# Linear attention followed by a spectral mix on one core: the first sixteen loads of q, k and V are written out in another order, and two of them are issued by ScalarE

## The chip, the cores and the metric

The kernel runs on one core of one Trainium2 chip. The metric is device time in microseconds (us) of one execution: before the change the median of three runs was 445.62 us, with 444.76 the lowest and 445.84 the highest.

## What is computed

Inputs are q, k and v of shape (batch 8, heads 8, sequence 576, 64), a projection `w_phi` (64 x 128), and the weights of the second part: `moe_w_r` and `moe_w_i` (64 modes of 512 x 512) and `moe_w_ch` (512 x 512). All are float32. The first part is attention with exponential features and no softmax:

```python
def phi(x):
    proj = x @ w_phi
    proj = proj - max(abs(proj))                 # over the 128 features
    return concatenate([exp(proj), exp(-proj)])  # 256 features
kv  = einsum('bhsf,bhsd->bhfd', phi(k), v);  z = phi(k).sum(sequence)
att = (phi(q) @ kv) / (phi(q) . z + 1e-6)
```

Its result, with the heads put side by side (512 columns), is the `x` of the second part. A real Fourier transform runs over the sequence; each of the first 64 modes is multiplied by its own complex 512 x 512 matrix; the inverse transform gives `y`; and with `u = x + y` the output is `u + relu(u @ w_ch)`, shape (8, 576, 512), float32.

## The kernel before

**Stages.** The attention part is a list `S` of 32 stages, each with two (batch, head) pairs, one on SBUF partitions 0 to 63 (the lower half) and one on 64 to 127 (the upper half). The main loop runs over n = 0 to 33, and in turn n it starts stage n, carries on stage n-1 and finishes stage n-2, so the three overlap. For a stage, q and k in bf16 are transposed on TensorE (`transp`, L196 and L199), copied out by VectorE (L205), projected (`feat_tok` L214, `feat_q` L223), their largest absolute value is taken by VectorE (`absmax`, L248), the exponentials are made by ScalarE (`exps` L255 to L263, `ekq` L270), V is scaled by GpSimd (`vscale`, L285 and L290), and matmuls and VectorE operations build the quotient into `xs_all` (L301 to L351).

**Loads of q, k and V.** V is loaded in float32 for every stage by SyncE (SP), through `load`, into four rotating buffers `vn` (L122 and L127). For stages 0 and 1 alone, `load` also brings q and k in float32 (`qn` and `kn`, two buffers each); `casts` (L154) turns those into bf16, on VectorE for stage 0 and on GpSimd for stage 1. A stage of this early kind takes two batches, so each of its tiles is loaded by two DMAs of 144 KB: the lower half first, then the upper. Sixteen such DMAs make up q, k and V of stages 0 and 1 and V of stages 2 and 3. From stage 2 on, q and k come in pairs of stages through `load_qk` (L138, L143): DMAs issued by GpSimd that cast to bf16 on the way.

**Weights.** The mode matrices come in 32 groups. `weights(k)` makes the four DMAs of a group (L169, L175; 512 KB as written in bf16, read as float32), each to one half of the partitions, lower half first, and GpSimd issues them. A list written by hand, `plan`, says how many of these DMAs and which `load_qk` GpSimd issues in each turn of the main loop, ahead of that turn's `vscale`. Three buffers rotate, so the issue of a group waits until the group three before it has been multiplied (`mode_mm`, L426 and L438). After the main loop, a second loop handles the remaining groups; then the inverse transform, the last matmul and the output follow.

**Order around the change.** The program order is written by hand and each engine works through its own list in order. Before the main loop it is: q and k of stage 0 on SP; the first group's list of weight DMAs; `setup` (ScalarE issues the two DMAs of `w_phi`, L486 and L487; GpSimd issues the first two weight DMAs, `load_qk` of stages 2 and 3, and the other two weight DMAs; VectorE and ScalarE make the Fourier table, L500 to L526; VectorE casts `w_phi` to `w2`, L527); V of stage 0, then q, k and V of stage 1 on SP; the casts of stage 0 on VectorE and of stage 1 on GpSimd, with small memsets between; the transposes of stage 0. V of stages 2 and 3 is loaded at the head of turns 0 and 1. DMAs of SP and ScalarE share eight completion semaphores in rotation, so the ninth of them waits until the first has landed, and so on.

Of the kernel before, what the change touches and what calls it, by code (L numbers as in the profile page):

```python
# [10 lines left out]
F32 = mybir.dt.float32  # L11
# [7 lines left out]
B_, H_, S_, D_ = 8, 8, 576, 64  # L19
# [7 lines left out]
def kernel(  # L27
# [11 lines left out]
    nc = tc.nc  # L39
# [43 lines left out]
    pa_in = pa_in_cm.__enter__()  # L83
# [7 lines left out]
    def qk_pair(pool, i):  # L91
        return [pool.tile([128, 2, 10, D_], BF16, name=f"{nm}2_{i}") for nm in "qk"]
# [3 lines left out]
    pa_first = pa_first_cm.__enter__()  # L96
# [4 lines left out]
    S = [dict(bs=(2 * i, 2 * i + 1), h=h, xt=1 - h) for h in range(2) for i in range(B_ // 2)]  # L101
    S += [dict(b=b, g=g, xt=g % 2) for g in range(1, H_ // 2) for b in range(B_)]
    N = len(S)
# [7 lines left out]
    after = [3] * 4 + [7] * 4 + [15] * 8 + [23] * 8 + [31] * 8  # L111
    W = {}

    def load(st, which="qkv"):
        for nm, src, bufs in (("q", q, 2), ("k", k, 2), ("v", v, 4)):
            if nm not in which or (nm != "v" and st["n"] >= 2):
                continue
            pool = pa_in if nm == "v" else pa_first
            t = pool.tile([128, 9, D_], F32, name=f"{nm}n", tag=f"{nm}n", bufs=bufs)
            if "bs" in st:  # L120
                for x in range(2):
                    nc.sync.dma_start(  # L122
                        t[64 * x:64 * x + 64],
                        src[st["bs"][x], st["h"]].rearrange("(p j) d -> p j d", j=9))
            else:
                b, g = st["b"], st["g"]
                nc.sync.dma_start(  # L127
                    t, src[b, 2 * g:2 * g + 2].rearrange("h (p j) d -> (h p) j d", j=9))
            st[nm] = t


    def load_qk(m):
        st = S[2 * m]
        for nm, src, t in zip("qk", (q, k), qk2s[m % 3]):
            if "bs" in st:
                for x in range(2):
                    b = st["bs"][x]
                    nc.gpsimd.dma_start(  # L138
                        t[64 * x:64 * x + 64, :, 0:9, :],
                        src[b:b + 3:2, st["h"]].rearrange("u (p j) d -> p u j d", j=9))  # L140
            else:
                b, g = st["b"], st["g"]
                nc.gpsimd.dma_start(  # L143
                    t[:, :, 0:9, :],
                    src[b:b + 2, 2 * g:2 * g + 2].rearrange("u h (p j) d -> (h p) u j d", j=9))
            for x in range(2):
                S[2 * m + x][nm + "b"] = t[:, x]

    def casts(st, eng, which="qk"):
        n = st["n"]  # L150
        for nm, t in zip("qk", qk2s[0]):
            if nm in which:
                st[nm + "b"] = t[:, n % 2]
                eng.tensor_copy(t[:, n % 2, 0:9, :], st[nm])  # L154

    def weights(k):
        g, gi = groups[k]
        W[k] = wt = {}
        for ri, w in ((0, moe_w_r), (1, moe_w_i)):
            for y in range(2):  # L160
                def issue(ri=ri, w=w, y=y):
                    if y == 0 and k == 0:
                        wt[ri] = Yacc.rearrange("p a e -> p (a e)").bitcast(BF16).rearrange(
                            "p (r m e) -> p r m e", r=2, m=8)[:, ri]
                    elif y == 0:
                        wt[ri] = pw.tile([128, 8, DMODEL], BF16, name=f"w{'ri'[ri]}", tag=f"w{ri}")
                    t = wt[ri][64 * y:64 * y + 64]
                    if gi >= 0:
                        nc.gpsimd.dma_start(  # L169
                            t.rearrange("p (m i) e -> p m (i e)", i=2),  # L170
                            w[8 * gi + y:8 * gi + 8:2, g * 128:(g + 1) * 128, :].rearrange(
                                "m (p i) e -> p m (i e)", i=2))
                    else:
                        m0 = 16 * (-1 - gi) + 8 * y
                        nc.gpsimd.dma_start(  # L175
                            t, w[m0:m0 + 8, g * 64:(g + 1) * 64, :].rearrange("m p e -> p m e"))
                due.append((k, issue))
# [130 lines left out]
    def kv_cp(st):  # L308
        kvzF = pa_mid.tile([128, 2, 130], BF16, name="kvzF", tag="kvzF")
        nc.scalar.copy(kvzF, st["kvz"][:, :, 0:130])  # L310
        st["kvzF"] = kvzF
# [248 lines left out]
    m_in = 2  # L560
    pa_last_cm = None
    with tc.manual_schedule():
        load(S[0], "qk")
        weights(0)
        k_in = 1
        setup()
        load(S[0], "v")
        load(S[1])
        casts(S[0], nc.vector)
        casts(S[1], nc.gpsimd, "q")  # L570
        for t in AAs:
            nc.gpsimd.memset(t[:, 0, :, 1152:1216], 1.0)
        for t in e2s:
            nc.gpsimd.memset(t[64:128, :, NCH - 1:NCH], 1.0)
        casts(S[1], nc.gpsimd, "k")

        pa_first_cm.__exit__(None, None, None)
        pa_last_cm = tc.tile_pool(name="pa_last", bufs=1)
        pa_last = pa_last_cm.__enter__()
        qk2s[2] = qk_pair(pa_last, 2)  # L580
        for t in qk2s[2]:
            nc.gpsimd.memset(t[:, :, 9, :], 0.0)
        transp(S[0], "q")
        transp(S[0], "k")
        for n in range(N + 2):
            cur = S[n] if n < N else None
            prev = S[n - 1] if 0 <= n - 1 < N else None
            old = S[n - 2] if 0 <= n - 2 < N else None
            nxt = S[n + 1] if n + 1 < N else None
            if n + 2 < N:  # L590
                load(S[n + 2])
            if cur:
                feat_tok(cur, "k", "pB")
                feat_q(cur)
            if psY is not None:
                mode_sum(k_out, psY)
                psY = None
                k_out += 1
            if cur:
                rem_mm(cur)  # L600
                absmax(cur, "k")
                absmax(cur, "rem")
                exps(cur, "q")
            if nxt:
                transp(nxt, "q")
            if prev:
                kv_mm(prev)
                kv_cp(prev)
            if cur:
                ekq(cur, "k")  # L610
            for c in plan[n - 1] if n else "":
                if c == "q":
                    load_qk(m_in)
                    m_in += 1
                elif c == "c":
                    nc.gpsimd.dma_start(wchb, moe_w_ch.rearrange("(dc p) e -> p dc e", p=128))
                else:
                    if not due:
                        assert k_in < max(k_out, 1) + NW
                        weights(k_in)  # L620
                        k_in += 1
                    issue_weights(1)
            if cur:
                vscale(cur)
            if n == 6:
                make_identity(nc, ident_f)
            if nxt:
                transp(nxt, "k")
            if cur:
                exps(cur, "k")  # L630
                exps(cur, "rem")
            if prev:
                num_mm(prev, 1)
                numer(prev, 0)
                num_mm(prev, 0)
                numer(prev, 1)
                numer(prev, 2)
            if old:
                x_mm(old)
            e = n - (N + 2 - N_EARLY)  # L640
            if e >= 0:
                sTe = flip_early(e)
            if cur:
                feat_tok(cur, "q", "pA")
                absmax(cur, "q")
                ekq(cur, "q")
            if n == 0:
                forward_matrix()
            if n in (1, 2):
                zeros(2 - n)  # L650
            if 10 <= n < 10 + NCH:
                inverse_matrix(n - 10)
            if n in (9, 15):
                zeros_late(1 if n == 9 else 0)
            if e >= 0:
                times_w_early(e, sTe)
            if k_out < len(at) and n == at[k_out]:
                assert after[k_out] + 2 <= n < (10, 18, 26, 99)[min(k_out // 4, 2) if k_out < 16 else 3]
                assert not due_of(k_out)
                psY = mode_mm(k_out)  # L660
# [147 lines left out]
    for n, (b, c, late) in enumerate(seq):  # L808
        u = dict(b=b, c=c, late=late == 1, half=c == 4, cut=n == 0, n=n,
                 tags=("T0", "T1") if n % 2 == 0 else ("T2", "T3"),  # L810
                 pool=(lambda: psumA) if n % 2 == 0 else (lambda: psum))
# [43 lines left out]
    with tc.manual_schedule():  # L855
        flip_x()
        flip_x()
        for k in range(k_out, 31):
# [8 lines left out]
            if yst is not None:  # L867
                if gi % 2 == 0:
                    sY = pb.tile([128, 4, 2, 128], BF16, name="sY", tag="sY")
                transposed(yst, sY, gi, (((0, 4), psum.tile([128, 4, 128], BF16, name="ptY",  # L870
                                                            tag="tr")),))
# [19 lines left out]
        for m, eng in ((-2, nc.sync), (-1, nc.gpsimd), (-3, nc.sync)):  # L891
            t, gi, a, b = Yst[m]
# [6 lines left out]
        st = [pb.tile([128, DMODEL], BF16, name=f"st{h}", bufs=1) for h in range(2)]  # L899
# [10 lines left out]
        for b, eng in ((1, nc.sync), (4, nc.gpsimd), (5, nc.sync), (6, nc.gpsimd),  # L910
                       (2, nc.sync), (7, nc.gpsimd), (3, nc.gpsimd)):
            j = b % 4
# [47 lines left out]
```

## Time and profile before

The profile is of one execution, which took 445.59 us, within 0.01% of the median; its span, from the first instruction to the last, is 443.8 us, and 1.8 us lie around it.

| what | value |
|---|---|
| time of the profiled execution | 445.59 us |
| span | 443.8 us |
| median of the runs | 445.62 us (444.76 to 445.84) |
| busy share: TensorE, VectorE, ScalarE, GpSimd | 70%, 66%, 61%, 49% |
| bytes written by DMA, packets | 97.86 MB, 60997 |
| queue q0 (DMAs issued by GpSimd) | 76.69 MB, 95.9% of 16 engines' span |
| queue q1 (DMAs issued by SP) | 20.35 MB, 13.3% |
| queue q10 (DMAs issued by ScalarE) | 0.07 MB, 0.1% |

PE is TensorE, PEld its weight loads, DVE is VectorE, ACT is ScalarE and POOL is GpSimd; SPq, ACTq and POOLq are their queues' instructions, such as the issue of a DMA. L122 is line 122 of the kernel. The profile counts a DMA's bytes as written: a DMA that casts float32 to bf16 reads twice what it writes. "DMA share" in the stretch tables adds up the time of packets over 16 engines, and packets of one engine overlap, so a full stretch shows more than 1.

### The profile page before, as it was taken

To read this page: it belongs to the slowest core of one execution; us is meant where nothing else is said; L and a number is where in the kernel's file an instruction comes from. 1 tells how busy PE (TensorE), PEld (TensorE's weight loads), DVE (VectorE), ACT (ScalarE), POOL (GpSimd) and SP (SyncE) were. 2 spreads that over 40 slices of the span, in tenths; PEclk is the share of its full clock that TensorE was granted. 3 is DMA by queue.
4 is the path that set the end of the run, shared out by engine and by line. 5 is a ranking of instruction groups with operands and counts; after the bars stand their busy time and mean duration, and the time that the engine had idled before them with its cause. 6 is when DMAs were issued, how large, how long until landed. Compare 5 with 4: busy or idle time off the path is not lost.

```text
span 443.8 us, 11840 instructions
## 1 busy us (share of the span) xinstructions
PE 310.9 (70%) x4981; PEld 201.5 (45%) x4981; DVE 293.7 (66%) x417; ACT 270.8 (61%) x567; POOL 218.1 (49%) x303
## 2 busy tenths in 40 slices
PE   0666667775767777677453767766897776789993
PEld 0455555554555655465342544433443333344441
DVE  4778879989888687878744796664232356363783
ACT  3676687886886875688633866663363254353762
POOL 6776448585566656547534554442222222200893
PEclk9999899899896596868966787888999699889997
DMA  8999999999999999999999999999999999993598
GB/s 190 243 228 218 220 228 217 229 218 218 230 221 223 221 233 221 223 233 222 223 220 222 222 222 211 211 212 211 211 211 211 211 211 211 211 207 74 183 363 328
DMA packets 60997, 97.86 MB, mean 221 GB/s; under 512 B 3936, under 2 KB 28992, under 8 KB 60944
## 3 DMA queue, kind: packets, MB, share of 16 engines
q0 software_dynamic: 51952, 76.69, 95.9%
q1 hardware_dynamic: 8832, 20.35, 13.3%
q8 instruction: 39, 0.64, 0.5%
q10 hardware_dynamic: 160, 0.07, 0.1%
q14 instruction: 14, 0.11, 0.1%
HBM read 163.64 MB, written 9.44 MB: 390 GB/s over the span
## 4 chain that ended last, share of the span: by engine, by line
DMA 55%; DVE 18%; PE 14%; issue 4%; ACT 4%; POOL 2%; ACTq 0%; SPq 0%; DVEq 0%; POOLq 0%
DMA wi<-in_moe_w_i_dram 35%; DMA wr<-in_moe_w_r_dram 9%; DMA k<-in_k_dram 8%; DVE mkq L248 7%; DVE nd L337 2%; DVE xs_all L351 2%; ACT AA L255 2%; DVE tB L330 2%; PE psB L785 2%; PE psB L778 2%; DMA kn<-in_k_dram 2%; PE psA L799 2%; PE ptr L199 1%; POOL vaug L285 1%; DMA fs<-in_w_phi_dram 1%
## 5 line engine op out<-in xcount | busy, mean ns | idle before, releaser
L285 POOL TENSOR_TENSOR vaug<-vn,ee 128x576 bf16<-128x576 f32 x64 | 72.7, 1156 | 45.7 <-ACT ee L270 43.6
L255 ACT ACTIVATE AA<-psT 128x1024 bf16<-128x1024 f32 x64 | 62.0, 1021 | 24.9 <-PE psT L223 24.2
L169 POOL DMA_DIRECT2D wr<-in_moe_w_r_dram x48 | 29.7, 620 | 78.4 <-PE psY L438 21.0
L277 ACT ACTIVATE e<-mkq 64x4 f32<-64x4 f32 (+1 forms) x128 | 26.3, 206 | 60.1 <-DVE mkq L248 57.7
L259 ACT ACTIVATE AA<-psk 128x1024 bf16<-128x1024 f32 x64 | 61.4, 1009 | 0.0
L169 POOL DMA_DIRECT2D wi<-in_moe_w_i_dram x48 | 29.9, 625 | 45.0 <-DMA wi<-in_moe_w_i_dram 13.5
L248 DVE TENSOR_REDUCE mkq<-psk 128x8 f32<-128x1024 f32 x32 | 38.7, 1211 | 0.7 <-PE psk L214 0.7
L248 DVE TENSOR_REDUCE mkq<-psq 128x8 f32<-128x1024 f32 x32 | 38.9, 1217 | 0.4 <-PE psq L214 0.3
L438 PE MATMUL psY<-wi,XT 128*32 128x512 bf16 x192 | 19.1, 477 | 26.1 <-DMA wi<-in_moe_w_i_dram 26.1
L707 ACT CAST xw<-psW 128x512 bf16<-128x512 f32 x34 | 19.8, 586 | 25.5 <-PE psW L705 25.2
L438 PEld LDWEIGHTS <-XT 128*32 128x32 bf16 x384 | 14.6, 173 | 45.8 <-issue 23.1
L705 PE MATMUL psW<-wchb,sT 128*128 128x512 bf16 x136 | 33.3, 389 | 0.0
L205 DVE COPY kT<-ptr 128x640 bf16<-128x640 bf16 x32 | 15.7, 492 | 25.3 <-PE ptr L199 25.3
L330 DVE TENSOR_TENSOR tB<-psNB,e 128x650 f32<-128x650 f32 x32 | 26.6, 832 | 8.8 <-PE psNB L320 8.4
L320 PEld LDWEIGHTS <-AA 128*128 128x128 bf16 x640 | 28.8, 110 | 7.6 <-issue 7.1
L697 DVE COPY sT<-pt 128x1024 bf16<-128x1024 bf16 x17 | 11.8, 692 | 30.5 <-PE pt L694 30.5
L223 PE MATMUL psT<-qT,w 64*128 64x512 bf16 x64 | 15.4, 471 | 23.4 <-DVE mkq L248 23.3
L199 PE MATMUL ptr<-ident_b,k 128*128 128x128 bf16 x160 | 18.1, 259 | 19.6 <-DVE qT L205 17.7
L351 DVE TENSOR_TENSOR xs_all<-nd,rden 128x640 bf16<-128x640 f32 x32 | 30.4, 951 | 1.1
L301 PE MATMUL kvz<-vaug,AA 64*128 64x65 bf16 x1152 | 28.8, 208 | 2.3 <-DVE Yacc L453 1.5
L337 DVE TENSOR_TENSOR nd<-psNA,tB 128x650 f32<-128x650 f32 x32 | 26.7, 835 | 3.8 <-DVE tB L330 0.5
L301 PEld LDWEIGHTS <-AA 64*128 64x128 bf16 x1152 | 24.5, 106 | 6.9 <-issue 2.3
(142 smaller groups left out, 726.6 us busy)
## 6 DMA issues: line engine op xcount, KB each, us to landing
wr<-in_moe_w_r_dram POOLq DMA_DIRECT2D x62, 512.0 KB, 18.9
wi<-in_moe_w_i_dram POOLq DMA_DIRECT2D x62, 512.0 KB, 18.7
out_dram<-of SPq DMA_DIRECT2D x15, 512.0 KB, 4.7
vn<-in_v_dram SPq DMA_DIRECT2D x24, 288.0 KB, 6.0
q<-in_q_dram POOLq DMA_DIRECT2D x12, 288.0 KB, 17.4
k<-in_k_dram POOLq DMA_DIRECT2D x12, 288.0 KB, 17.6
vn<-in_v_dram SPq DMA_DIRECT2D x16, 144.0 KB, 7.0
Yacc<-in_moe_w_r_dram POOLq DMA_DIRECT2D x2, 512.0 KB, 8.7
```

Of the source, the lines that this page charges most:

```text
L169: nc.gpsimd.dma_start(t.rearrange("p (m i) e -> p m (i e)", i=2), w[8 * gi + y:8 * gi + 8:2, g * 128:(g + 1) * 128, :].rearrange("m (p i) ...
L248: nc.vector.tensor_reduce(out=o, in_=i, axis=AX.X, op=ALU.max, apply_absolute_value=True)
L255: nc.scalar.activation(AA[:, 0, ab, 0:1024].rearrange("f (x j p) -> f j x p", j=2, p=64), st["psT"].rearrange("f j (x p) -> f j x p", p=64 ...
L259: nc.scalar.activation(AA[:, 1, ab, 0:1024].rearrange("p (c j f) -> p j c f", c=4, j=2), st["psk"], ACT.Exp, scale=sc)
L285: nc.gpsimd.tensor_tensor(out=vaug[:, ab, :, 0:64], in0=st["v"], in1=ee[:, ab, :].unsqueeze(2).to_broadcast([128, 9, D_]), op=ALU.mult,)
L301: nc.tensor.matmul(kvz[:, hh, ab * 65:(ab + 1) * 65], lhsT=AA[r, 1, ab, 128 * j:128 * j + 128], rhs=vaug[r, ab, j, :], start=(j == 0), sto ...
L320: nc.tensor.matmul(p[:, hh, 65 * c:65 * c + 65], lhsT=AA[:, 0, ab, x:x + 128], rhs=kvzF[:, hh, ab * 65:(ab + 1) * 65], start=True, stop=True,)
L330: nc.vector.tensor_tensor(out=tB, in0=st["psNB"], in1=e2.unsqueeze(3).to_broadcast([128, 2, NCH, 65]), op=ALU.mult,)
L337: nc.vector.tensor_tensor(out=nd, in0=st["psNA"], in1=st["tB"], op=ALU.add)
L351: nc.vector.tensor_tensor(out=xo, in0=nd[:, :, :, 0:64], in1=rden.to_broadcast([128, 2, NCH, 64]), op=ALU.mult,)
L438: nc.tensor.matmul(psY[32 * j:32 * j + 32, :], lhsT=XT[:, 16 + 32 * ri:48 + 32 * ri, 32 * i + 4 * gi + j], rhs=wt[ri][:, 2 * j + i, :], st ...
L705: nc.tensor.matmul(ps, lhsT=sT[:, x, dc, :], rhs=wchb[:, dc, :], start=(dc == 0), stop=(dc == 3))
```

## The change

The sixteen first loads are written out in one function, called where `load(S[0], "qk")` stood, ahead of everything else. The lower half of q and then of k of stage 0 goes to SP, and the upper halves of the same two to ScalarE, ahead of its two DMAs of `w_phi`. Then SP issues all remaining upper halves (V of stage 0; q, k and V of stage 1; V of stages 2 and 3), and after them the lower halves in the same order. The sixteen DMAs are the same as before in size, source and destination; 14 are now SP's and 2 ScalarE's. The calls of `load` for stages 0 to 3 go; from stage 4 on V is loaded as before. On TensorE, VectorE and GpSimd the order of instructions is the same in both kernels.

```diff
+    def first_loads():
+        for n in range(4):
+            for nm, bufs in (("q", 2), ("k", 2), ("v", 4)):
+                if nm == "v" or n < 2:
+                    pool = pa_in if nm == "v" else pa_first
+                    S[n][nm] = pool.tile([128, 9, D_], F32, name=f"{nm}n", tag=f"{nm}n", bufs=bufs)
+
+        def half(eng, n, nm, x):
+            src = dict(q=q, k=k, v=v)[nm]
+            eng.dma_start(S[n][nm][64 * x:64 * x + 64],
+                          src[S[n]["bs"][x], S[n]["h"]].rearrange("(p j) d -> p j d", j=9))
+
+        for nm in "qk":
+            half(nc.sync, 0, nm, 0)
+            half(nc.scalar, 0, nm, 1)
+        for x in (1, 0):
+            for n, nm in ((0, "v"), (1, "q"), (1, "k"), (1, "v"), (2, "v"), (3, "v")):
+                half(nc.sync, n, nm, x)
...
     with tc.manual_schedule():
-        load(S[0], "qk")
+        first_loads()
         weights(0)
         k_in = 1
         setup()
-        load(S[0], "v")
-        load(S[1])
         casts(S[0], nc.vector)
...
-            if n + 2 < N:
+            if 4 <= n + 2 < N:
                 load(S[n + 2])
```

More of the change, by code (lines that the diff above doesn't have):

```diff
@@ L112, with load @@
     W = {}
[L114 to L126, printed above, removed]
-                nc.sync.dma_start(
-                    t, src[b, 2 * g:2 * g + 2].rearrange("h (p j) d -> (h p) j d", j=9))
-            st[nm] = t
+    def load(st):
+        st["v"] = t = pa_in.tile([128, 9, D_], F32, name="vn", tag="vn", bufs=4)
+        if "bs" in st:
+            for x in range(2):
+                nc.sync.dma_start(
+                    t[64 * x:64 * x + 64],
+                    v[st["bs"][x], st["h"]].rearrange("(p j) d -> p j d", j=9))
+        else:
+            b, g = st["b"], st["g"]
+            nc.sync.dma_start(
+                t, v[b, 2 * g:2 * g + 2].rearrange("h (p j) d -> (h p) j d", j=9))
+    def first_loads():
[14 more added lines that the diff above has]
+                half(nc.sync, n, nm, x)
     def load_qk(m):
```

## The prediction

> **What bounds the kernel now.** I read the page's slices (section 2) first, then the chain of work that ended last, then a table of short stretches.
>
> ```profile
> DMA  8999999999999999999999999999999999993598
> GB/s 190 243 228 218 220 228 217 229 218 218 230 221 223 221 233 221 223 233 222 223 220 222 222 222 211 211 212 211 211 211 211 211 211 211 211 207 74 183 363 328
> q0 software_dynamic: 51952, 76.69, 95.9%
> ...
> 385.86 19.60 DMA wi<-in_moe_w_i_dram
> 405.51 0.69 PE psY L438 x5
> ```
>
> The DMA engines are full from the first slice to the 35th; the slice at 400 us (74 GB/s) is the first empty one. The last weight DMA lands at 405.5 us and TensorE goes on at once; the 38.3 us behind it (443.8 - 405.5) are output work that this change does not touch. So the end is: when the stream starts, plus its bytes at its rate, plus any time in which it is empty, plus 38.3. The stretches show where it is not full:
>
> ```profile
> 2.00:3.00 1.00, 0.00 (x0) 0.00 (x0) 0.00 (x0) 1.00 (x1) 0.93 (x3) 1.00 0.69 184
> 3.00:4.00 1.00, 0.00 (x0) 0.00 (x0) 0.56 (x3) 0.26 (x1) 0.81 (x6) 1.00 0.88 103
> 7.00:10.00 3.00, 0.74 (x10) 0.50 (x10) 0.65 (x2) 1.49 (x2) 1.28 (x2) 1.00 1.15 282
> 13.00:19.00 6.00, 3.64 (x39) 2.15 (x37) 4.15 (x7) 4.92 (x10) 4.73 (x12) 1.00 1.15 258
> 380.00:385.00 5.00, 4.48 (x36) 2.35 (x35) 1.12 (x3) 3.10 (x4) 1.22 (x2) 0.96 1.12 211
> ```
>
> The last two columns are DMA share and GB/s written. Nothing moves before 2 us; from 2 to 4 us the share is 0.69 and 0.88 where 1.12 is full; after that it is never under 1.10. The sixteen loads add no bytes and lose none, so only two things can move the end: the gap at 2 to 4 us, and a new gap made by GpSimd issuing a DMA too late. GpSimd's issues stand behind its casts of stage 1, so I read the start on the timeline (start, duration, what):
>
> ```profile
> 0.75 1.47 SPq L122 DMA_DIRECT2D qn<-in_q_dram  x2
> 0.75 0.56 ACTq L486 DMA_DIRECT2D fs<-in_w_phi_dram  x1
> ...
> 7.31 0.35 DVE L527 CAST w<-fs 128x128 bf16<-128x128 f32 x1 [0.62 <-DMA fs<-in_w_phi_dram]
> ...
> 10.08 0.46 DVE L154 CAST k<-kn 128x576 bf16<-128x576 f32 x1 [2.12 <-DMA kn<-in_k_dram]
> ...
> 13.72 0.66 POOL L154 CAST q<-qn 128x576 bf16<-128x576 f32 x1 [5.44 <-DMA qn<-in_q_dram]
> ...
> 15.30 0.66 POOL L154 CAST k<-kn 128x576 bf16<-128x576 f32 x1 [0.43 <-DMA kn<-in_k_dram]
> ...
> 18.68 1.25 POOL L138 DMA_DIRECT2D q<-in_q_dram  x2
> ```
>
> **Stage 0 (removed from SP, added to ScalarE).** Upper q is issued at 0.75 us instead of 1.41, beside the lower. In the DMA rows SP's first load lands 3.0 us after its issue (3.7 us), its second 6.0 after (7.4), its third and fourth at 8.1 and 10.0. Now q0's first packets come at 2.8 us (its two issues begin at 1.28 and 2.11), so what both queues bring before that is free. Of a second 144 KB half (147 KB) in place of 32 KB of `w_phi`, some 115 KB more can move in the gap; at the full rate of 422 KB/us read (2 x 211) that is **0.3 us gained**. Ends: nothing, and the whole gap, 1.1 us (two stretches at 411 KB/us, from 2 x 411 less 355 KB moved, q0 counted as read). I take 0.3, since only one half is added.
>
> The Trainium skill ("DMA: Bandwidth & Descriptors", section "Issuing engines are not separate DMA queues") says that DMAs of several issuers run on the same 16 engines and that two issuers save only issue time. By it the 0.3 us would be nothing and the time 445.6.
>
> ScalarE issues two DMAs more, at 0.56 to 0.61 us each: its table load moves from 1.98 to about 3.2 us and ends at 4.5, and it waits for VectorE until 5.83 in any case (its idle row is 2.57 us there): nothing. `w_phi` becomes the third and fourth of its queue. Its last half landed at 7.2 us as the second; the nearest row for a fourth is 10.0. I take 8.3. Then VectorE casts w2, q and k in a row (0.35 + 0.47 + 0.46) and is done at 9.6 us against 10.5 now, because upper k is no longer the fourth load. With 10.0 it is done at 11.3, +0.8. Either way stage 0 waits for stage 1 a little later.
>
> **Stage 1 (moved back).** Before, q and k of stage 1 were complete with SP's 8th and 10th loads, which landed at 13.6 and 15.15 us. Now they are complete with SP's 10th and 11th, and ScalarE has two of its own. SP's 11th and 13th loads now land at 16.2 and 18.2. If ScalarE's two halves cost SP nothing, k is complete at 16.2 (+1.0); if they push it back by their full number, at 18.2 (+3.1). I take **+1.5**: from 4 to 7 us SP's queue moved just 0.20 MB and q0 0.47, so a third queue takes mostly from q0. V of stage 0 (SP's 9th) is there before GpSimd's two casts are done, so L285 is not held further. Everything behind L154 on GpSimd (memsets, L285, L290, then `load_qk` at L138) and on TensorE (transposes of stage 1, and behind them the psq matmuls of stage 0) goes 1.5 us later, and the chain from 15.3 to 105 us consists of VectorE, TensorE and ScalarE pieces with almost no wait, so they stay 1.5 us late until it meets the DMAs.
>
> **Does the lateness reach the stream?** Twice GpSimd issues with little cover. (a) L138 at 18.68 us: q0's four weight and four q/k DMAs before it are 2.69 MB, and the window to 24.5 us shows them just done:
>
> ```profile
> q0 software_dynamic: 2673, 2.68, 66.3%
> ```
>
> and (b) L175 at 68.66 us, on GpSimd's timeline:
>
> ```profile
> 68.66 1.42 POOL L175 DMA_DIRECT2D wr<-in_moe_w_r_dram  x2
> ```
>
> An issue's first packet comes 1.6 us after it starts (1.28 to 2.85 at the beginning), so cover is 24.5 - 18.68 - 1.6 = 4.2 us, less 0.7 for V of stage 4 (0.295 MB), which also comes later: 3.5. For (b), the DMA before it (k, 60.46, 13.7 us to land) lands at 74.15; landing follows the last packet by 1.8 us (24.5 and 26.3 for q0's eighth), so q0 runs dry at 72.3; new packets come at 70.3. Cover is 2.0 us. So +1.5 costs nothing at either. From (b) on each issue finds older DMAs that land 7 us or more later (7 to 18), and lateness is swallowed. Sum on the profiled time: 445.59 - 0.3 + 0 = **445.3 us**, the profiled execution and the median being 0.03 apart.
>
> **Rivals.** *The stream runs dry (slower).* Place: the issue at 68.66 us, behind the stage work that k of stage 1 delays. It decides from a lateness of 2.0 us; above, each us of lateness costs one. With +3.1 it is 1.1 less the 0.3 gained: 446.4; with k three halves later still (0.9 each in the landing rows), 448. For: SP's order puts three more loads ahead of k's lower half. Against: the same row of 0.20 MB, and V of stage 8 may fill part.
>
> *Halves get in each other's way.* Before, SP's loads alternate lower and upper; now six or more of one half follow each other while q0's second weight DMA (landing 7.6 to 13.2) writes the upper half too. If one half took no more than the 211 GB/s of the weight-only stretch, where each DMA writes one half, then 4.5 us at 211 instead of 270 lose 1.0 us, and the lower halves beside q0's q/k another 0.5: 446.3 to 446.8. Against: the row 7:10 has 282 GB/s, with q0's upper half and SP's upper k in it, though lower V too. The Trainium skill ("SBUF — State Buffer", section "Door 1: The DMA port swizzle") says that 64 partitions reach half of the 16 DMA ports, which is this mechanism; the row of 282 speaks against it as far as it goes.
>
> *The start gains more.* The whole gap closes (1.1 us) and the thin stretch 13:19 (258 against 282 GB/s in 6 us: 0.5 us) fills: 444.0. For: the order gives each half's queue its own run. Against: nothing issues earlier than 0.75 us, and most of the gap is waiting for first packets.
>
> That the change does not do what it says is out: SP has 14 loads and ScalarE 2, in the order written.
>
> **Numbers.** Forecast 0.58, runs dry 0.20, halves collide 0.10, start gains more 0.12. A measurement of this kernel can tell about 0.3% from no change, 1.3 us: below 444.3 is faster, above 447.0 slower. Faster: the last rival, 0.12. Slower: half of the dry stream (0.10, lateness over 3.5 us), half of the collision (0.05, where a late k empties the stream on top) and 0.02 of the forecast's own spread: 0.17. The rest, 0.71, is the same. The range 444.2 to 447.1 leaves out some 0.2: the best start and a stream dry for over 1.5 us.
>
> **What would show it.** After: q of stage 0 complete before 5 us; L527 at 8 to 9; L154 for k on VectorE done near 9.6; on GpSimd near 16.8; L138 near 20; L175 of the fifth `weights` near 70; never a stretch under 1.1 of DMA share after 4 us; last weight DMA at 405.2. The prediction is wrong if a stretch near 24 or 72 us shows q0 empty, if the rate at 7 to 19 us falls towards 211, or if 2 to 4 us fills.

## The result, and the profile after

The changed kernel takes 448.62 us (median of 7 runs, 447.21 to 450.03) and the kernel before 445.84 in the same comparison (7 runs, 444.76 to 446.30): a ratio of 1.0066, 95% interval 1.0048 to 1.0083. It is **2.8 us slower**, above the forecast range. The profiled execution took 448.31 us, its span is 446.5.

The slices of the changed kernel and the end of its chain of waits:

```profile
DMA  8999999999999999999999999999999999994598
GB/s 187 229 222 220 218 221 185 219 226 222 217 221 234 221 228 225 222 233 222 221 221 222 222 221 211 211 211 211 211 211 211 211 211 211 211 211 86 181 360 328
...
388.51 19.60 DMA wi<-in_moe_w_i_dram
408.15 0.69 PE psY L452 x7
```

The end is built as before: the last weight DMA lands, TensorE goes on at once, and 38.4 us of output follow (38.3 before). But it lands at 408.1 us instead of 405.5, so the stream is 2.65 us late: nearly the whole span's 2.7. The seventh slice moves 185 GB/s where its neighbours move about 220, though its DMA digit still reads 9: packet times overlap (a full stretch here reads 1.18 to 1.25), so a slice of 11 us can hide the loss of 2 us of transfer. A table of short stretches shows it (last columns: granted clock, DMA share, GB/s written), first the start, then 70 to 78 us:

```profile
2.00:3.00 1.00, 0.00 (x0) 0.00 (x0) 0.00 (x0) 0.00 (x0) 0.93 (x3) 1.00 0.80 249
3.00:4.00 1.00, 0.00 (x0) 0.00 (x0) 0.56 (x3) 0.72 (x1) 0.81 (x6) 1.00 0.76 115
10.00:13.00 3.00, 0.74 (x10) 0.61 (x11) 1.32 (x4) 0.00 (x0) 0.00 (x0) 1.00 1.25 210
13.00:19.00 6.00, 2.50 (x28) 1.69 (x27) 2.18 (x4) 3.46 (x6) 1.08 (x5) 1.00 1.17 245
70.00:72.00 2.00, 2.00 (x42) 1.64 (x39) 1.90 (x3) 2.00 (x6) 1.93 (x5) 1.00 1.13 194
72.00:74.00 2.00, 1.46 (x41) 1.03 (x41) 1.93 (x4) 0.36 (x2) 0.96 (x2) 1.00 0.68 179
74.00:76.00 2.00, 1.48 (x49) 1.10 (x50) 2.00 (x3) 1.54 (x5) 2.00 (x4) 1.00 0.68 88
76.00:78.00 2.00, 0.90 (x33) 0.87 (x26) 1.47 (x4) 1.98 (x6) 0.28 (x2) 1.00 1.23 201
```

The same stretches before the change:

```profile
70.00:72.00 2.00, 1.36 (x51) 1.07 (x48) 2.00 (x3) 1.93 (x5) 1.44 (x3) 1.00 1.18 264
72.00:74.00 2.00, 1.35 (x32) 1.29 (x32) 1.47 (x4) 1.98 (x6) 0.85 (x1) 1.00 1.25 202
74.00:76.00 2.00, 1.93 (x50) 1.68 (x54) 1.83 (x4) 2.00 (x6) 2.00 (x4) 1.00 1.24 206
76.00:78.00 2.00, 1.23 (x36) 0.58 (x20) 2.00 (x3) 0.41 (x3) 2.00 (x4) 1.00 1.24 207
```

From 72 to 76 us the DMA share is 0.68, where it was 1.25 and 1.24. By 24 us the stream is 0.9 us behind the stream of before, by 70 us 1.2, by 77 us 3.3 (bytes moved, q0's counted as read, over 415 KB/us); 2.65 us are left when the last weight DMA lands. GpSimd's timeline has the reason, from the casts of stage 1 to the fifth group of weights:

```profile
17.83 0.67 POOL L168 CAST q<-qn 128x576 bf16<-128x576 f32 x1 [9.54 <-DMA qn<-in_q_dram]
...
19.03 0.66 POOL L168 CAST k<-kn 128x576 bf16<-128x576 f32 x1
...
22.41 1.25 POOL L152 DMA_DIRECT2D q<-in_q_dram  x2
...
69.33 2.27 POOL L299 TENSOR_TENSOR vaug<-vn,ee 128x576 bf16<-128x576 f32 x2 [4.80 <-ACT ee L284]
...
73.32 1.42 POOL L189 DMA_DIRECT2D wr<-in_moe_w_r_dram  x2 [1.04 <-PE psY L440]
```

The cast of k is 3.7 us later (15.30 before), L152 3.7 (18.68), the fifth group 4.7 (68.66). The last adds a wait of 1.04 us for TensorE to have read the weight buffer, which was free before.

### The profile page after: what moved, and what is told of

The parts are those of the page before. It is cut to its first block, busy times and chain, and to the rows that moved or that the text cites. A ratio compares the mean times of both kernels' runs of the same rounds, so it can differ in the third digit from the quotient of the medians.

```text
span 446.5 us, 11840 instructions
## 1 busy us (share of the span) xinstructions
PE 311.2 (70%) x4981; PEld 202.9 (45%) x4981; DVE 291.1 (65%) x417; ACT 271.1 (61%) x567; POOL 216.6 (49%) x303
## 4 chain that ended last, share of the span: by engine, by line
DMA 55%; DVE 19%; PE 14%; ACT 6%; issue 3%; POOL 1%; ACTq 0%; SPq 0%; DVEq 0%; POOLq 0%
DMA wi<-in_moe_w_i_dram 39%; DMA wr<-in_moe_w_r_dram 8%; DVE mkq L262 7%; DMA k<-in_k_dram 4%; DVE nd L351 2%; DVE xs_all L365 2%; ACT AA L269 2%; PE psB L797 2%; DMA fs<-in_w_phi_dram 2%; PE psB L790 2%; DVE tB L344 2%; DMA qn<-in_q_dram 2%; PE psA L811 2%; PE ptr L213 1%; DVE qT L219 1%
## 5 line engine op out<-in xcount | busy, mean ns | idle before, releaser
L452 PE MATMUL psY<-wi,XT 128*32 128x512 bf16 x192 | 17.8, 445 | 25.9 <-DMA wi<-in_moe_w_i_dram 25.9
L717 PE MATMUL psW<-wchb,sT 128*128 128x512 bf16 x136 | 35.2, 405 | 0.0
L213 PE MATMUL ptr<-ident_b,k 128*128 128x128 bf16 x160 | 17.5, 253 | 18.4 <-DVE qT L219 17.2
L237 PE MATMUL psT<-qT,w 64*128 64x512 bf16 x64 | 14.7, 449 | 21.9 <-DVE mkq L262 21.9
L210 PE MATMUL ptr<-ident_b,q 128*64 128x128 bf16 x320 | 18.1, 255 | 15.2 <-DVE q L168 11.9
L365 DVE TENSOR_TENSOR xs_all<-nd,rden 128x640 bf16<-128x640 f32 x32 | 27.5, 858 | 1.1
## 6 DMA issues: line engine op xcount, KB each, us to landing
k<-in_k_dram POOLq DMA_DIRECT2D x12, 288.0 KB, 16.9
```

What stands on the lines that cost most here:

```text
L365: nc.vector.tensor_tensor(out=xo, in0=nd[:, :, :, 0:64], in1=rden.to_broadcast([128, 2, NCH, 64]), op=ALU.mult,)
L452: nc.tensor.matmul(psY[32 * j:32 * j + 32, :], lhsT=XT[:, 16 + 32 * ri:48 + 32 * ri, 32 * i + 4 * gi + j], rhs=wt[ri][:, 2 * j + i, :], st ...
L717: nc.tensor.matmul(ps, lhsT=sT[:, x, dc, :], rhs=wchb[:, dc, :], start=(dc == 0), stop=(dc == 3))
```

## The experiments

Theory L: the lateness of stage 1 empties the weight stream near 72 us. Rival S: ScalarE's two loads do it (a thin start, `w_phi` behind them). Rival H: loads that write the same half of the partitions as q0 hinder each other. Line numbers shift between kernels; the names of what is done do not. "Work by 24 us" is bytes moved, q0's counted as read: 7.90 MB before (2 x 2.59 + 2.65 + 0.07), 7.53 after (2 x 2.55 + 2.07 + 0.36). Each experiment was measured beside the kernel before, whose median was 445.3 to 445.8 us; a ratio is to that median. The landings, issues and bytes of a run are those of its one profiled execution.

**e1, the order alone.**

```diff
-            half(nc.scalar, 0, nm, 1)
+            half(nc.sync, 0, nm, 1)
```

> The new order alone: SyncE issues all sixteen loads (both halves of q and k of stage 0 first, then all upper halves, then all lower ones), ScalarE only w_phi, as before the change. Theory L (stage 1's lateness lets the weight stream run dry near 72 us): k of stage 1 is SyncE's 13th load, lands near 18.2 us instead of 15.15, GpSimd's cast of it ends near 19; GpSimd's fifth group of weights is issued 3 us late or more, q0 is empty for 1 to 2 us near 73 us, and the time is 1.3 to 2.5 us over before. Rival S (ScalarE's two loads, w_phi behind them and the shared completion semaphores do it): stage 1 is at most 1 us late, the stream stays full and the time is within 0.5 us of before. Rival H (halves of one kind hinder each other): no empty stretch, but a rate below 240 GB/s written from 7 to 19 us, and 1 to 1.5 us over before, all of it lost by 24 us.

449.42 us, ratio 1.0082 (1.0063 to 1.0101). k of stage 1 lands at 19.0 us, the fifth group is issued at 73.91, the last weight DMA lands at 408.5. So ScalarE is not needed for the loss (against S). But 0.85 us are lost by 24 us before anything is empty, which L does not explain. This profiled execution is the slowest of its six (450.62 us): 2 us of its excess lie behind the stream, where the granted clock from 410 to 415 us is 0.66.

**e2, ScalarE alone.** The order of SyncE's list is the old one.

```diff
-        for x in (1, 0):
-            for n, nm in ((0, "v"), (1, "q"), (1, "k"), (1, "v"), (2, "v"), (3, "v")):
+        for n, nm in ((0, "v"), (1, "q"), (1, "k"), (1, "v"), (2, "v"), (3, "v")):
+            for x in (0, 1):
                 half(nc.sync, n, nm, x)
```

> ScalarE issues the upper halves of q and k of stage 0 ahead of w_phi, and SyncE the other fourteen in the old order (lower, upper, tile by tile). Theory L: k of stage 1 is SyncE's 8th load instead of 10th and lands by 15 us; w_phi lands near 11 us as after the change, so stage 0 is some 1.5 us late, which is under the cover of 2 us: no empty stretch near 72 us, time within 0.7 us of before. Rival S: the lateness is ScalarE's doing, so 3 us or more late at GpSimd's fifth group, an empty stretch near 72 us, 2 to 3 us over before. Rival H: alternating halves, so like before.

447.93 us, ratio 1.0046 (1.0029 to 1.0062): slower than L allowed. Yet the fifth group is issued at 68.76, nothing is empty near 72 us, and the last weight DMA lands at 405.8, 0.3 late. The rest of its loss is behind the stream: in the stretch 405 to 415 us the granted clock is 0.78 and 0.88 (5 us each) where it was 1.00, and the z matmuls take 3.1 us instead of 1.7.

**e3, `w_phi` ahead of ScalarE's halves.**

```diff
+        nc.scalar.dma_start(fs[0:64, 0:128], w_phi)
+        nc.scalar.dma_start(fs[64:128, 0:128], w_phi)
         for nm in "qk":
             half(nc.sync, 0, nm, 0)
             half(nc.scalar, 0, nm, 1)
```

> The changed kernel, with ScalarE's two w_phi loads ahead of its two upper halves. Theory L: w_phi lands before 8 us, stage 0 is no later than before, but q and k of stage 1 are still SyncE's 10th and 11th loads and land 3 us late; empty stretch near 73 us, 2 to 3 us over before, within 0.7 us of the changed kernel. Rival S, in the form that w_phi's landing at 11 us is the cause: the lateness and the empty stretch go, time within 0.5 us of before. Rival H: as the changed kernel.

449.86 us, ratio 1.0078 (1.0052 to 1.0104). `w2` is cast at 6.6 us instead of 11.2, and nothing is won: the fifth group is issued at 73.21 and the stream is thin from 74 to 76 us. `w_phi`'s landing is not the cause. Stage 0 as a whole is no earlier, since ScalarE's halves of q and k now land at 9.3 and 11.4 us (3.5 and 8.6 in the changed kernel) and VectorE is done with it at 12.0 (12.2). The start is worse, too: the work by 24 us is 6.93 MB, 2.3 us behind before.

**e4, lower halves first.**

```diff
-        for x in (1, 0):
+        for x in (0, 1):
```

> The changed kernel with all lower halves ahead of all upper halves in SyncE's list (ScalarE as in the changed kernel). Theory L: the same number of loads stands ahead of q and k of stage 1, so the same lateness, empty stretch near 73 us and time as the changed kernel, within 0.7 us. Rival H: which half meets which of q0's weight DMAs is exchanged (q0 writes the lower half first), so the work moved by 24 us differs by 0.5 us or more from that of the changed kernel, and with it the time.

448.47 us, ratio 1.0050 (1.0028 to 1.0072): as the changed kernel, as L says. But k of stage 1 lands at 16.9 instead of 18.7, and the work by 24 us is 0.17 MB (0.4 us) more, just under what H asked for. Its profiled execution (446.45 us) is the fastest of its seven.

**e5, stage 1 ahead of V.**

```diff
         for x in (1, 0):
-            for n, nm in ((0, "v"), (1, "q"), (1, "k"), (1, "v"), (2, "v"), (3, "v")):
+            for n, nm in ((1, "q"), (1, "k")):
+                half(nc.sync, n, nm, x)
+        for x in (1, 0):
+            for n, nm in ((0, "v"), (1, "v"), (2, "v"), (3, "v")):
                 half(nc.sync, n, nm, x)
```

> The changed kernel, but q and k of stage 1 (upper halves, then lower) go ahead of all V in SyncE's list; ScalarE as in the changed kernel. Theory L: q and k of stage 1 are SyncE's 5th and 6th loads and land by 13 us, GpSimd's casts wait for nothing new, the fifth group of weights is issued within 1 us of 68.7, there is no empty stretch near 73 us, and the last weight DMA lands at 406.5 us or before (408.1 in the changed kernel); time 1.5 to 3 us under the changed kernel. Rival S (ScalarE's loads and the thin first 24 us they make): what was lost by 24 us stays lost, last weight DMA at 407.5 or later. Rival H: halves still come in runs, so no gain over the changed kernel.

447.17 us, ratio 1.0035 (1.0014 to 1.0057): 1.6 us over the kernel before, where the changed kernel is 2.8 over, so the gain is a little less than L gave. In the profile the fifth group is issued at 69.38 and the last weight DMA lands at 405.4, as L has it; but this profiled execution (446.04 us) is the fastest of twelve, and the 1.6 us that remain in the median are not seen in it.

**e7, a delay and nothing else** (12 repeats in the small one, 24 in the large; the kernel before, no load moved).

```diff
+        for _ in range(12):
+            nc.gpsimd.memset(AAs[0][:, 0, :, 1152:1216], 1.0)
         casts(S[1], nc.gpsimd, "k")
```

> The kernel before, with 12 repeated small memsets on GpSimd ahead of its cast of k of stage 1; no load is moved. It only makes stage 1 some 1.6 us later. Theory L: under the cover of 2 us near 72 us, so no empty stretch, and last weight DMA within 0.5 us of 405.5; time within 0.7 us of before. Rivals S and H: no change at all.

> The kernel before, with 24 repeated small memsets on GpSimd ahead of its cast of k of stage 1; no load is moved. It makes stage 1 some 3.7 us later, as the change does. Theory L: the fifth group of weights is issued 4 to 5 us late, q0 is empty for about 2 us near 73 us, the last weight DMA lands 1.7 to 2.5 us later than 405.5, time 1.5 to 2.5 us over before. Rivals S and H: the loads are as before, so the stream is too, time within 0.7 us of before.

Large: 449.76 us, ratio 1.0086 (1.0063 to 1.0109), last weight DMA at 408.4, thin near 74 us and also near 24, where L138 is issued at 23.88, 5.2 us late. The delay came out larger than meant (5.2 us at the cast instead of 3.7), and with it the loss: 4.2 us over the kernel before, where L gave 1.5 to 2.5. Small: 447.23, ratio 1.0033 (1.0015 to 1.0051), where nothing was expected. Short stretches of the small delay:

```profile
70.00:72.00 2.00, 1.22 (x42) 0.73 (x27) 2.00 (x3) 0.43 (x3) 1.90 (x4) 1.00 0.98 214
72.00:74.00 2.00, 1.64 (x51) 1.23 (x51) 2.00 (x2) 1.90 (x6) 1.73 (x3) 1.00 0.66 111
```

and of the large one:

```profile
24.00:26.00 2.00, 2.00 (x41) 1.46 (x40) 1.88 (x6) 1.92 (x5) 2.00 (x5) 1.00 0.41 66
72.00:74.00 2.00, 1.91 (x51) 1.33 (x49) 1.93 (x4) 1.23 (x5) 1.90 (x5) 1.00 0.89 149
74.00:76.00 2.00, 1.04 (x21) 0.65 (x22) 2.00 (x3) 1.09 (x5) 2.00 (x4) 1.00 0.57 145
```

Lateness alone, with no load moved, makes the loss, so L is shown. The small delay issues the fifth group 2.3 us late (70.94), and by 77 us the stream is 1.4 us behind before (it was level at 70): the cover there is some 0.9 us, not 2.

**e8, the changed kernel with q and k ahead of the fifth group.**

```diff
-    plan = [... "ww", "q", "wwww", "qwww", ...]
+    plan = [... "ww", "q", "qwwww", "www", ...]
```

> The changed kernel, with the load of a pair of stages' q and k moved from turn 8 of the hand-written plan to turn 7, ahead of the fifth group's weights, so that GpSimd has 576 KB (as written) to give the stream while it waits for a weight buffer. Theory L: the empty stretch near 73 us shrinks by 1 us or more (q's first packets at about 73.5 instead of 75), last weight DMA near 407, time 0.7 to 1.5 us under the changed kernel. Rivals S and H: the loss is elsewhere, time within 0.5 us of the changed kernel.

448.50 us, ratio 1.0062 (1.0038 to 1.0087): no gain over the changed kernel, where L had 0.7 to 1.5 us. q is issued at 72.59, right behind GpSimd's other work of that turn and only 0.7 us before the weights went out in the changed kernel; the weights follow at 74.03, 0.7 us later. By 77 us the stream is 3.2 us behind, as without the edit (3.3). Not a repair.

**e9, the kernel before with stage 1 ahead of V of stage 0.**

```diff
-        load(S[0], "v")
-        load(S[1])
+        load(S[1], "qk")
+        load(S[0], "v")
+        load(S[1], "v")
```

> The kernel before, with q and k of stage 1 loaded ahead of V of stage 0; all sixteen loads stay on SyncE, lower and upper halves alternating. Theory L: k of stage 1 lands near 13.5 us instead of 15.15; V of stage 0 near 14.5, in time for GpSimd; stage 1 is up to 1.5 us earlier, the cover near 72 us is larger, the stream is never thin there, and the last weight DMA lands 0 to 0.5 us before 405.5; time from 0.7 us under to 0.3 us over before. Rivals S and H: no lateness is involved, time as before.

445.84 us beside 445.67, ratio 1.0005 (0.9986 to 1.0023). The fifth group is issued 1.4 us earlier and the stream ends at 405.0; the time cannot be told from before.

**e10, e2 with `w_phi` first.** e2's edit and e3's together.

> ScalarE issues w_phi and then the upper halves of q and k of stage 0; SyncE the other fourteen in the old order. e2 (ScalarE's loads ahead of w_phi) lost 2 us though its profiled stream ended just 0.3 us late. If w_phi landing at 9.6 us and more was the cause there, this kernel is within 0.7 us of before. If sharing the eight completion semaphores and a thinner start are the cause, the work moved by 24 us is 0.3 us or more behind before and the time 0.5 us or more over it.

446.19 us, ratio 1.0012 (0.9996 to 1.0028). Work by 24 us 0.4 us behind; the start does not gain from ScalarE's loads here either.

**e2 and e5, profiled again.**

> A second look at ScalarE alone. In the first look the stream ended at 405.8 us, 0.3 later than before, but the output work behind it took 2.2 us longer, with the granted TensorE clock at 0.5 from 407.8 to 411.2 us. If the dip of the clock belongs to this kernel it is there again, with 40 us or more behind the last weight DMA; if it falls there by chance, this look may have 38.3 us there and a stream that ends later.

> A second look at the changed kernel with stage 1's loads ahead of V. Its first look was its fastest execution (446.04 us, median 447.2). If executions differ by the landing of the first loads, this one has a later stage 1 or a thin stretch near 72 us; if by the clock behind the stream, a dip of the granted clock between 405 and 445 us.

e2: 447.50 us, but now with no dip of the clock behind the stream; the stream ends at 406.9 and lost 1.6 us from 318 to 335 us, where GpSimd waited 11.2 and 5.1 us for TensorE to free weight buffers (9.9 and 3.0 before). From 323 to 328 us it wrote 179 GB/s (209 before). The same place is thin in e10 (189 GB/s; 0.8 us lost from 318 to 335 us). e5: 445.52 us, stream ending at 405.6, full near 72 us, but 0.6 us lost at that later place.

**e11, e1 with the first group's weights upper half first.** No load of q, k or V is touched.

```diff
-            for y in range(2):
+            for y in ((1, 0) if k == 0 else (0, 1)):
```

> e1 (the new order, all on SyncE), with the first group's weight DMAs issued upper half first instead of lower half first; nothing else. In e1 SyncE's run of upper halves was served from 8 to 14 us beside q0's upper-half weights, at 203 GB/s written or little more, and its packets took 183 ns in 10 to 14 us instead of 133. Rival H, now as a second cause: q0 writes the lower half in that time, so the stretch 8 to 14 us goes back to 250 GB/s or more, packets take 105 to 135 ns, and the work moved by 24 us is 0.5 to 1 us ahead of e1; k of stage 1 lands 0.5 us or more earlier. Without H (theory L alone): the same rates as e1. In both the stream still runs dry near 73 us, since k of stage 1 stays SyncE's 13th load; time 0.5 to 1.5 us under e1 with H, within 0.5 us of it without.

447.42 us, ratio 1.0046 (1.0030 to 1.0063): 2.1 us over the kernel before, where e1 is 3.6 over. DMA queues from 8 to 14 us (packets, MB, share of 16 engines), of before, of e1 and of e11:

```profile
DMA packets 1120, 1.59 MB, mean 265 GB/s; under 512 B 142, under 2 KB 679, under 8 KB 1120
...
q1 hardware_dynamic: 551, 1.02, 59.3%
```

```profile
DMA packets 927, 1.31 MB, mean 218 GB/s; under 512 B 111, under 2 KB 564, under 8 KB 927
...
q1 hardware_dynamic: 458, 0.84, 69.5%
```

```profile
DMA packets 1203, 1.72 MB, mean 286 GB/s; under 512 B 150, under 2 KB 722, under 8 KB 1203
...
q1 hardware_dynamic: 600, 1.11, 55.6%
```

A packet of q1 takes 103 ns before (59.3% of 16 x 6 us over 551), 146 in e1 and 89 in e11. (The 183 and 133 ns of the expectation are the packets over 2 KB alone, from 10 to 14 us; those take 105 in e11.) The same loads in the same order take a third longer for the same bytes (218 against 286 GB/s) when q0 writes the same half: H is shown as a second cause. k of stage 1 lands at 16.6 us in e11 and 19.0 in e1, and the work by 24 us is 8.12 MB against 7.55, 1.4 us more. The stream still runs dry (70 to 74 us): one that is ahead empties sooner.

**e12, the changed kernel with the same swap.**

> The changed kernel with the first group's weight DMAs issued upper half first. With H: the run of upper halves now meets q0's upper half from 3 to 8 us, early, and its lower half after it, so the thin place moves forward, and the work moved by 24 us differs from the changed kernel's by 0.3 us or more; the empty stretch near 73 us stays, within 1 us in its length. Without H: as the changed kernel.

447.92 us, ratio 1.0046 (1.0023 to 1.0070); work by 24 us 0.22 MB (0.5 us) more, k of stage 1 at 18.0 (0.7 us earlier), fifth group at 72.29, thin near 73 us. In the changed kernel this swap gives back little.

**e13, halves opposed on purpose**, all on SyncE.

```diff
+        for n, nm, x in ((0, "q", 0), (0, "q", 1), (0, "k", 1), (0, "k", 0),
+                         (1, "q", 0), (1, "k", 0), (0, "v", 0), (1, "v", 0),
+                         (1, "q", 1), (1, "k", 1), (0, "v", 1), (2, "v", 0),
+                         (1, "v", 1), (3, "v", 0), (2, "v", 1), (3, "v", 1)):
+            half(nc.sync, n, nm, x)
```

> All sixteen loads on SyncE, w_phi first on ScalarE, in an order that puts each half beside the other half of q0: upper q and k of stage 0 while q0 writes its first lower half, then lower k, q1, k1, V0, V1 while it writes the upper half (7.6 to 13 us), then q1, k1 and V0 upper, then the rest. With H and L: 8 to 14 us at 270 GB/s or more, work moved by 24 us 0.3 us or more ahead of before, k of stage 1 at 15 to 15.5 us, no empty stretch near 73 us, last weight DMA at 405.3 or earlier; time 0 to 1 us under before. Without H: rates and time as before.

445.14 us beside 445.30, ratio 0.9989 (0.9977 to 1.0001): clearly under the changed kernel, and against before at most a trace. From 8 to 14 us it moves 1.72 MB, as e11 (1.59 before), and k of stage 1, SyncE's 10th load as before, lands 0.8 us earlier; the stream ends at 405.1.

**The changed kernel, profiled again.**

> A second look at the changed kernel. Theory L: the empty stretch between 70 and 77 us is there again, of 1.3 to 3 us, with the fifth group of weights issued 3 us or more later than 68.7.

449.16 us: fifth group at 72.90, thin from 71 to 76 us (1.7 us lost), last weight DMA at 408.9. The same picture.

Put together, by profiled executions (us); "behind" is the work by 77 us against before, over 415 KB/us, negative where it is ahead:

| kernel | k of stage 1 landed | fifth group issued | behind at 77 us | last weight DMA landed |
|---|---|---|---|---|
| e9 | 12.7 | 67.2 | -0.2 | 405.0 |
| e10 | 14.5 | 68.2 | 0.4 | 405.7 |
| e2, again | 14.9 | 68.4 | 0.3 | 406.9 |
| before | 15.2 | 68.7 | 0 | 405.5 |
| e2 | 14.0 | 68.8 | 0.3 | 405.8 |
| e5, again | 11.9 | 68.9 | 0.4 | 405.6 |
| e13 | 14.4 | 69.0 | -0.1 | 405.1 |
| e5 | 11.7 | 69.4 | 0.4 | 405.4 |
| e7 small | 14.7, cast 2.1 later | 70.9 | 1.4 | 407.0 |
| e4 | 16.9 | 71.1 | 1.6 | 406.5 |
| e11 | 16.6 | 71.7 | 1.8 | 406.4 |
| e12 | 18.0 | 72.3 | 2.4 | 407.5 |
| after, again | 18.3 | 72.9 | 3.2 | 408.9 |
| e3 | 18.4 | 73.2 | 3.5 | 409.3 |
| after | 18.7 | 73.3 | 3.3 | 408.1 |
| e7 large | 14.3, cast 5.2 later | 73.8 | 4.0 | 408.4 |
| e1 | 19.0 | 73.9 | 4.0 | 408.5 |
| e8 | 18.6 | 74.0 | 3.2 | 408.5 |

A fifth group issued up to 69.4 costs 0.2 us or less near 72 us. Later, each further microsecond counts: in the nine rows from e7 small to e1 the lateness against 68.7, less what the stream is behind at 77 us, is 0.8 to 1.4 us, whatever the cause of the lateness was. That is the cover. (e8 stands apart: it put q and k ahead of the weights.) At the landing of the last weight DMA, between a third (e11) and nearly all (e3) of the lateness is left; what gives the rest back is not shown.

## Why the prediction was wrong

- **What bounds the kernel: right.** Stream, its holes, and 38.3 us behind it. The hole that opened is the one named, at the fifth group of weights, by the rival of the dry stream; its mechanism was given 0.20.
- **"I take +1.5": the step that failed.** k of stage 1 came 3.6 us later, above the +3.1 taken as the upper end, and the fifth group 4.7 us later, since GpSimd also waited 1.0 us for a weight buffer there. The choice of +1.5 rested on the reading that a third queue takes mostly from q0, so that ScalarE's halves cost SyncE little. They cost it nearly their full number: with them the last half of k is SyncE's 11th load and lands at 18.7 us, without them (e1) it is the 13th and lands at 19.0; where SyncE's runs are faster (271 GB/s from 8 to 14 us in e4, 286 in e11) it lands at 16.9 with them (e4) and at 16.6 without (e11). That is the +3.1 that the text named and put aside. The rest is collisions of halves, which move the same landing by 2.3 us (e1 against e11, with nothing else changed) and which the text priced as lost rate of the stream and never put into the landing of stage 1, where they count most. How the 3.6 us divide is not shown: the swap that gains 2.3 us in e1 gains 0.7 in the changed kernel (e12). The two rivals were one case.
- **The row read against H.** The 282 GB/s from 7 to 10 us hold lower halves beside q0's upper one. The row with one half on both queues is e1's: 218 GB/s from 8 to 14 us, near the 211 of the weight-only stretch. The Trainium skill ("SBUF — State Buffer", section "Door 1: The DMA port swizzle") has 64 partitions reach half of the ports; the runs agree with it as far as 218 against 286 GB/s shows.
- **"Cover is 2.0 us": too much.** It is 0.8 to 1.4 (the table above). At the first place the text took off 0.7 us because V of a later stage comes late too and cannot fill; at the second it did not, though V of stage 8 shifts just the same, and even counted it as a help. With the 0.7 taken off, 1.3 us are left, as measured. This error alone would have cost little: +1.5 against this cover is 0.1 to 0.7 us.
- **"0.3 us gained" at the start: no.** 2 to 3 us moves 249 GB/s instead of 184, but 4 to 6 us is thinner (share 1.09 instead of 1.17), and by 6 us the kernel is 0.06 MB behind. Loads of two issuers bring nothing here (e10: 0.4 us behind by 24 us). The Trainium skill ("DMA: Bandwidth & Descriptors", section "Issuing engines are not separate DMA queues") has it so; the runs agree.
- **`w_phi` at 8.3: it landed at 11.1**, past the nearest row, too. Stage 0 was done at 12.2 instead of 9.6. That is not what dried the stream: in e11 stage 0 is done at 9.8, earlier than before (10.5), and the stream runs dry all the same.
- **The collision after the change.** What it loses by 24 us (0.9 us in the changed kernel) does not add to the end: a stream that is behind runs dry later. e3, 2.3 us behind by 24 us, and e11, 0.5 us ahead, have much the same cover in the table (1.0 and 1.2 us).
- **"Never under 1.10" before the change: nearly.** In stretches of 2 us, 136 to 138 us reads 1.08 and 160 to 162 us 1.09, at 272 and 261 GB/s; neither is a hole.

Open: why e2 is 2.1 us slower in the median, and e5 1.6 us, though neither runs dry near 72 us. e2's two profiles lost the time in different places, once behind the stream with a low clock and once near 326 us. The second place is thin in e10 and in e5's second profile, too, and loses next to nothing in the profiles of kernels in which SyncE issues all the halves. So ScalarE's two loads may have a cost of their own beside the dry stream; whether they cause this one, and how much of the changed kernel's 2.8 us it would be, is not shown.

## What to carry to other kernels

Where one queue feeds a kernel from end to end, list for each issue how long the queue lasts without it; the smallest of these, not the share of busy time, says what a delay upstream costs, and everything that shifts with the delay has to be taken out of the cover. In these runs a half of the partitions was a resource of its own: set transfers of different queues against each other's halves. And when two rivals feed the same number, price them together.

## What the runs showed of the hardware that was not expected

Packets of one queue were slowed by another queue's writes to the same 64 partitions: 146 ns against 89, with the engines' total at 218 against 286 GB/s written. And the granted clock falls to 0.5 for some microseconds at places that differ from run to run. Where no wait hides it, it costs time: 2 us behind the stream when the z matmuls met it (3.1 us in e2 and 3.4 in e1, instead of 1.7).
